# Batched set attention and an MLP on one core: h @ w_in of later batches as one product on four column groups

## The chip, the cores and the metric

The kernel runs on one core of a Trainium2 chip, in one launch. The metric is the device time of an execution in microseconds; for the kernel before it is the median of three runs.

## What is computed

Four batches of 12480 rows go through two attention steps over 32 inducing vectors, and then through an MLP with a gelu in its sigmoid form:

```python
B, N, m, C = (4, 12480, 32, 128)

def mab(q, kv):
    s = scale * (q @ kv.transpose(0, 2, 1))
    s = s - s.max(-1, keepdims=True)
    a = np.exp(s)
    a /= a.sum(-1, keepdims=True) + 1e-09
    return a @ kv
h = mab(I, x)            # (B, 32, 128)
out = mab(x, h)          # (B, 12480, 128)

h1 = out @ w_in          # w_in: 128 x 2048
g = h1 * (1.0 / (1.0 + np.exp(-1.702 * h1)))
result = g @ w_out       # w_out: 2048 x 128
```

## The kernel before

The last product of the second attention and the first of the MLP are joined: the kernel forms `hw = h @ w_in` once a batch (32 x 2048, as four tiles of 512 columns, `hw[b, 0]` to `hw[b, 3]`), and the MLP's first product is then the attention weights times `hw`. To keep float32 precision at the speed of a fast float32 product, weights and `hw` are split into a high and a low part. A tile of `hw` has 128 partitions: the 32 rows of h four times over, the upper two groups the high part, the lower two the low part. A tile of weights, `st`, has the high part in groups 0 and 2 and the low part in 1 and 3, so one product over 128 partitions adds up all four combinations.

**Tiling.** A batch is six super-blocks of 2048 tokens and a remainder of 192 (`sups`, numbers 0 to 6). A block is 512 tokens of one super-block, or the remainders of two batches together (`work`, lines 663 to 683): 98 blocks. Each has eight steps, 784 in all, numbered from 0. A step `first(i)` (684) is two products `ph<-st,hw` on PE, `g` on ACT (gelu), `hi` on ACT or DVE, by which of them has less queued, and `lo` on DVE. `second(i, c)` (711) is three products `pso` with w_out, which follow their step by a lag of up to 12 halves of a step (6 to 12, `LAG`). `ph` has two buffers, so the `ph` products of a step need the gelu of two steps before.

**Order.** Nothing is scheduled by the compiler: each engine runs its instructions in the order in which the program writes them. The main loop (783 to 815) writes one step, then the due `second`s, and then lets two generators run up to their next `yield`: the attention of a later batch (`rest`, line 809), and the laying out of a super-block's weights (`back`). `hop(n)` yields n times, so one yield is one step. `attention(b)` of batch b writes, in this order: the first scores, their maximum and exponentials, the weighted sum, `hT` (the 32 columns of h, four times side by side), the second scores in pairs of super-blocks (`second_products`, 452; `second_out`, 462: a transpose and a reduction on DVE, a subtraction on POOL), first of four super-blocks and then of three, and after each of the two groups their exponentials on ACT. Odd batches begin with their remainder.

Exponentials and gelu need different tables on ACT, so each group of exponentials stands between two table loads. Behind such a group the attention yields LUMP. The main loop then writes `second`s until only 6 halves are left, which gives PE products that need nothing of ACT:

```python
if i < n and next(rest, None) is LUMP:
    while len(under_way) > LAG[0]:
        second(*under_way.pop(0))
    lag, last = LAG[0], i
```

`weights_of(b, s)` (535) normalises the exponentials of a super-block, splits them and copies them to `st` by 32 transfers on SP. Line 772 says from which step on this is due (`begin`): 14 steps before the super-block's first block, earlier where one follows closely. `lay_out` (776) starts it, and where the exponentials are not written by then it runs the attention on:

```python
key = turns.pop(0)
while key not in es:
    next(rest)
return weights_of(*key), key
```

For the first super-block that is laid out in batches 1, 2 and 3 from its own attention's first group, `begin` is 174, 378 and 566.

**Around the change.** `h_w_in(b, c)` (520) is one quarter of `hw`: one product of `hT` (128 columns, h four times) with 512 columns of w_in, a copy to the high part on ACT, a subtraction for the low part on 64 partitions on DVE. For batch 0 the start-up does it; for batches 1 to 3 the list `products` puts the four quarters at single steps shortly before the batch's first block. `phw` is the pool of the tiles of `hw`, `pt` that of the transposed weights. Most instructions carry line 46, that of a helper that records them, so the rows are read by the names of tiles.

Of the kernel before, what the change touches and what calls it, by code (L numbers as in the profile page):

```python
# [8 lines left out]
F32 = mybir.dt.float32  # L9
I32 = mybir.dt.int32  # L10
F32R = mybir.dt.float32r
# [5 lines left out]
P = 128  # L17
# [33 lines left out]
def width(ap):  # L51
    return math.prod(ap.shape[1:])
# [3 lines left out]
def set_attention_then_moe(ctx: ExitStack, tc, xT, x, indT, w_in, w_out, outT):  # L56
    nc = tc.nc
# [11 lines left out]
    dve = Meter(nc.vector, lambda out, *a, **k: 70 + 1.04 * width(out))  # L69
    act = Meter(nc.scalar, scalar_cost)  # L70
    pe_ = Meter(nc.tensor, tensor_cost)
    M = indT.shape[1]
    G = P // M
    DFF = w_in.shape[1]
    NCH = DFF // P
    NG = NCH // 2
    NTOT = xT.shape[1]
    B = 4
# [9 lines left out]
    NS = len(sups)  # L88
# [4 lines left out]
    pe = ctx.enter_context(tc.tile_pool(name="pe", bufs=EB))  # L93
    pt = ctx.enter_context(tc.tile_pool(name="pt", bufs=7))
    pst = ctx.enter_context(tc.tile_pool(name="pst", bufs=G))
    phw = ctx.enter_context(tc.tile_pool(name="phw", bufs=7))
    psm = ctx.enter_context(tc.tile_pool(name="psm", bufs=3))
    ps_h = ctx.enter_context(tc.tile_pool(name="ps_h", bufs=2, space=PSUM))
    ps_o = ctx.enter_context(tc.tile_pool(name="ps_o", bufs=2, space=PSUM))
    ps_a = ctx.enter_context(tc.tile_pool(name="ps_a", bufs=2, space=PSUM))  # L100
# [19 lines left out]
    w_in_sb = const.tile([P, DFF], F32, name="w_in_sb")  # L120
# [4 lines left out]
    hw = {}  # L125
    hTs = {}
    first_h = []
# [21 lines left out]
    def hop(n=4):  # L149

        for _ in range(n):
            yield
# [45 lines left out]
    def attention(b):  # L198

        start = b == 0  # L200
# [44 lines left out]
        def maximum(n):  # L245

            mx1 = psm.tile([P, 1], F32, tag="mx1", name="mx1")
            dve.tensor_reduce(mx1, mx[:, 0:n], axis=AX.X, op=ALU.max)
            yield from wait()
            pa = ps_a.tile([P, 512], F32, tag="pa", name="pa")  # L250
            pe_.matmul(pa[0:1, 0:P], mx1, ident, start=True, stop=True)
            yield
            row = psm.tile([1, G, M], F32, tag="row", name="row")
            dve.tensor_reduce(
                row[:, 0, :], pa[0:1, 0:P].rearrange("p (g m) -> p m g", g=G), axis=AX.X, op=ALU.max
            )
            for j in range(1, G):
                dve.tensor_copy(row[:, j, :], row[:, 0, :])
            yield from wait()
            pa = ps_a.tile([P, 512], F32, tag="pa", name="pa")  # L260
            pe_.matmul(pa[:, 0:1], row.rearrange("p g m -> p (g m)"), one, start=True, stop=True)
            yield
            nmx = psm.tile([P, 1], F32, tag="nmx", name="nmx")
            dve.tensor_scalar(nmx, pa[:, 0:1], -scale, None, op0=ALU.mult)
            yield from wait(2)
            return nmx
# [20 lines left out]
        def weigh(pa, s, xn, i, n):  # L287

            t0, g, w = sups[s]
            q = 32 * g  # L290
            for kk in range(w // 32):
                j = i % G
                pe_.matmul(
                    pa[32 * j:32 * j + 32, 0:P], aTs[s][0:q, kk, :], xn[0:q, kk],
                    start=(i < G), stop=(i >= n - G),
                )
                i += 1
            return i
# [9 lines left out]
        def again(s):  # L308

            if s < NS - 1:  # L310
                load_xT(b, s)

        def blocks(some):
            return sum(sups[s][2] // 32 for s in some)

        if start:
# [36 lines left out]
            def whole():  # L353
                found.append((yield from maximum(NS)))

            whole = whole()
            i = 0
            next(whole)
            spin(SPIN[0])
            for s in range(ES):  # L360
                i = weigh(h1, s, turned[s], i, blocks(range(ES)))
# [17 lines left out]
            i = 0  # L379
            for s in range(ES, NS):  # L380
                if s not in turned:
                    turned[s] = turn_x(b, s)
                i = weigh(h2, s, turned[s], i, blocks(range(ES, NS)))
# [10 lines left out]
        else:  # L394
# [16 lines left out]
            pa = ps_a.tile([P, 512], F32, tag="pa", name="pa")  # L411
# [3 lines left out]
            i = 0  # L415
            for s in range(NS):
# [7 lines left out]
                i = weigh(pa, s, xn, i, blocks(range(NS)))  # L424
# [10 lines left out]
        pa = ps_a.tile([P, 512], F32, tag="pa", name="pa")  # L435
# [16 lines left out]
        def second_products(s):  # L452
            t0, g, w = sups[s]
            pa = ps_a.tile([P, 512], F32, tag="pa", name="pa")
            for j in range(g):
                pe_.matmul(
                    pa[32 * j:32 * j + 32, 0:w], hT[:, 0:M], xts[b, s][:, j * w:(j + 1) * w],
                    start=True, stop=True,
                )
            return pa  # L460

        def second_out(s, pa):

            t0, g, w = sups[s]
            q = 32 * g
            e, slot = take("e", s)
            k = w // 32
            e = e[:, 0:w].rearrange("p (k m) -> p k m", m=M)
            dve.transpose(e[0:q].rearrange("p k m -> p (k m)"), pa[0:q, 0:w])
            m2 = psm.tile([P, BLK], F32, tag="m2", name="m2")  # L470
            dve.tensor_reduce(m2[0:q, 0:k], e[0:q], axis=AX.X, op=ALU.max)
            yield
            eng = dve if start and s == 0 else nc.gpsimd
            eng.tensor_sub(e[0:q], e[0:q], m2[0:q, 0:k].unsqueeze(2).broadcast_to([q, k, M]))  # L474
            yield
            return e, slot
# [8 lines left out]
        if start:  # L485
            for s in range(2):
                pa = second_products(s)
                if s + XB < NS:
                    again(s + XB)
                yield  # L490
                mine[s] = yield from second_out(s, pa)
                exponentials(s, mine[s])
            halves = [h_w_in(b, c) for c in range(DFF // 512)]
            for part in halves:
                next(part)
            spin(SPIN[1])
            yield from weights_of(b, 0)
            for part in halves:
                for _ in part:
                    yield  # L500
            act.activation(warm, one, AF.Gelu_apprx_sigmoid)
            ready.append(True)
        yield
        for some in (turn[2:],) if start else (turn[0:4], turn[4:]):
            yield from hop(20 if start else 8)
# [13 lines left out]

    def h_w_in(b, c):  # L520

        if b == 0:
            if c % 2 == 0:
                first_h.append(ps_h.tile([P, 2, 512], F32, tag="ph", name="ph"))
            pa = first_h[-1][:, c % 2]
        else:
            pa = ps_a.tile([P, 512], F32, tag="pa", name="pa")
        pe_.matmul(pa, hTs[b], w_in_sb[:, c * 512:(c + 1) * 512], start=True, stop=True)
        yield
        t = phw.tile([P, 512], F32R, tag="hw", name="hw")  # L530
        act.copy(t, pa)
        dve.tensor_sub(t[P // 2:P], pa[P // 2:P], t[P // 2:P].bitcast(F32))
        hw[b, c] = t

    def weights_of(b, s):

# [43 lines left out]
    def run(gen):  # L580
        for _ in gen:
            pass
# [78 lines left out]
    first_block = {}  # L661
# [94 lines left out]
            yield from attention(b)  # L756

    n = len(work) * NG

    products = []  # L760
    for b in range(1, B):
        f = first_block[b, NS - 1 if b % 2 else 0] * NG
        products += [(f + at, b, c) for c, at in enumerate((-6, -4, -2, 1) if b % 2 else (-7, -5, -3, -1))]
    rest = attentions()
    act.t = dve.t = pe_.t
    back = part = laid = None
    stores = []
    under_way = []
    turns.pop(0)
# [13 lines left out]
    i, lag, last = 0, LAG[0], 0  # L783
    while i < n or under_way:
        now[0] = i
        if i < n:
            if back is None and turns and i >= begin[turns[0]]:
                back, laid = lay_out()
            while back is not None and first_block[laid] * NG <= i:
                run(back)  # L790
                back = None
                if turns and first_block[turns[0]] * NG <= i:
                    back, laid = lay_out()
            first(i)
            if part is not None:
                run(part)
                part = None
            if products and products[0][0] == i:
                part = h_w_in(*products.pop(0)[1:])
                next(part)  # L800
            under_way += [(i, 0), (i, 1)]
            i += 1
        else:
            lag = 0
        while len(under_way) > lag:
            second(*under_way.pop(0))
        while stores and (stores[0][0] <= i or not under_way):
            nc.sync.dma_start(*stores.pop(0)[1:])
# [4 lines that stand above are left out]
        if lag < LAG[1] and i - last >= EXTRA:  # L813
            lag, last = lag + 1, i
        if back is not None and next(back, 0) == 0:
            back = None
# [33 lines left out]
```

## Time and profile before

| | us |
|---|---|
| median of three runs | 1630.17 (1630.16 to 1631.4) |
| the profiled execution | 1632.7 |
| its span, first to last instruction | 1630.9 |
| PE busy in it | 1591.0 (98%) |
| DVE busy | 1386.9 (85%) |
| ACT busy | 1331.5 (82%) |
| POOL busy | 197.9 (12%) |

The profile's page gives busy times of each engine (PE is the matrix engine, PEld its weight loads, DVE the vector, ACT the scalar, POOL the GpSimd engine, SP the one that issues the transfers), the chain of work that ended last, and groups of instructions. A row of the timeline has the start and the duration in us; instructions of a kind that follow each other are merged in it (x2, x8), and the idle time of the engine just before stands in brackets with what ended it. A product of two plain float32 operands is recorded as two instructions, one of the fast format as one. Times of steps below are program positions; what happens when is read from the timeline.

### The profile page before, as it was taken

To read this page: it belongs to the slowest core of one execution; us is meant where nothing else is said; L and a number is where in the kernel's file an instruction comes from. 1 tells how busy PE (TensorE), PEld (TensorE's weight loads), DVE (VectorE), ACT (ScalarE), POOL (GpSimd) and SP (SyncE) were. 2 spreads that over 40 slices of the span, in tenths; PEclk is the share of its full clock that TensorE was granted. 3 is DMA by queue.
4 is the path that set the end of the run, shared out by engine and by line. 5 is a ranking of instruction groups with operands and counts; after the bars stand their busy time and mean duration, and the time that the engine had idled before them with its cause. 6 is when DMAs were issued, how large, how long until landed. Compare 5 with 4: busy or idle time off the path is not lost.

```text
span 1630.9 us, 21863 instructions
## 1 busy us (share of the span) xinstructions
PE 1591.0 (98%) x7737; PEld 1233.0 (76%) x7737; DVE 1386.9 (85%) x1515; ACT 1331.5 (82%) x1513; POOL 197.9 (12%) x134
## 2 busy tenths in 40 slices
PE   6799999999999999999999999999999999999999
PEld 3477777787777877777766877777777888888887
DVE  7788978988889887888888988878988888889886
ACT  5488888888878878987888878988788888888885
POOL 4311100103101011011120110110121101101100
PEclk9899999999999999999999999999999999999999
DMA  8304219503042112850205101671301011011010
GB/s 338 104 16 175 64 37 203 120 19 97 19 142 76 43 39 56 184 126 20 91 14 202 40 27 39 136 183 40 97 16 42 25 39 46 20 39 46 22 44 20
DMA packets 81947, 126.66 MB, mean 78 GB/s; under 512 B 11632, under 2 KB 50096, under 8 KB 75696
## 3 DMA queue, kind: packets, MB, share of 16 engines
q1 hardware_dynamic: 81840, 125.26, 27.1%
q8 instruction: 63, 1.03, 0.3%
q14 instruction: 44, 0.36, 0.1%
HBM read 74.10 MB, written 25.56 MB: 61 GB/s over the span
## 4 chain that ended last, share of the span: by engine, by line
PE 88%; DVE 4%; ACT 3%; DMA 2%; issue 2%; SPq 1%; POOL 0%; ACTq 0%; DVEq 0%; POOLq 0%
PE pso L46 62%; PE ph L46 22%; PE pa L46 4%; DMA xt<-in_xT 2%; DVE lo L46 2%; ACT g L46 1%; ACT hi L46 1%; SPq L575 1%; DVE sm L46 1%; DVE hi L46 0%; DVE e L46 0%; DVE m L46 0%; DVE hw L46 0%; DVE t L46 0%; ACT s L46 0%
## 5 line engine op out<-in xcount | busy, mean ns | idle before, releaser
L46 DVE TENSOR_TENSOR lo<-g,hi 128x1024 fp32r<-128x1024 f32 (+1 forms) x784 | 983.1, 1268 | 134.4 <-ACT hi L46 122.0
L46 ACT ACTIVATE g<-ph 128x1024 f32<-128x1024 f32 (+1 forms) x784 | 804.3, 1030 | 232.2 <-PE ph L46 119.0
L46 PE MATMUL pso<-hi,wl 128*128 128x512 f32 (+1 forms) x1568 | 623.7, 398 | 0.0
L46 PE MATMUL pso<-hi,wh 128*128 128x512 f32 (+1 forms) x1568 | 617.3, 394 | 0.0
L46 PE MATMUL pso<-lo,wh 128*128 128x512 f32 (+1 forms) x1568 | 616.6, 393 | 0.0
L46 PE MATMUL ph<-st,hw 128*128 128x512 f32 x1536 | 491.2, 401 | 6.8 <-ACT hi L46 2.7
L46 ACT ACTIVATE hi<-ph 128x1024 fp32r<-128x1024 f32 (+1 forms) x464 | 474.1, 1022 | 0.0
L46 PEld LDWEIGHTS ph<-st,hw 128*128 128x128 f32 x1536 | 282.2, 188 | 100.5 <-issue 18.7
L46 PEld LDWEIGHTS pso<-lo,wh 128*128 128x128 f32 x1568 | 294.5, 188 | 73.2 <-issue 2.2
L46 PEld LDWEIGHTS pso<-hi,wl 128*128 128x128 f32 x1568 | 295.3, 188 | 70.4 <-issue 2.9
L46 PEld LDWEIGHTS pso<-hi,wh 128*128 128x128 f32 x1568 | 294.9, 188 | 70.3
L46 DVE CAST hi<-g 128x1024 fp32r<-128x1024 f32 x320 | 239.6, 749 | 77.0 <-ACT g L46 76.7
L547 POOL TENSOR_TENSOR e<-e,sm 128x512 f32<-128x512 f32 (+1 forms) x27 | 44.0, 1631 | 1132.8 <-DVE sm L46 1132.8
L46 ACT COPY ob<-pso 128x512 f32<-128x512 f32 (+1 forms) x98 | 58.0, 591 | 17.5 <-PE pso L46 17.5
L474 POOL TENSOR_TENSOR e<-e,m 128x512 f32<-128x512 f32 (+1 forms) x27 | 42.5, 1574 | 180.4 <-DVE m L46 135.8
L551 POOL TENSOR_TENSOR e<-e,ah 128x512 f32<-128x512 f32 (+1 forms) x27 | 49.5, 1834 | 2.2
L46 PE MATMUL pa<-xt,indT_sb 128*32 128x512 f32 x192 | 27.6, 676 | 17.2 <-DMA xt<-in_xT 17.2
L46 ACT ACT_TABLE_LOAD x28 | 35.9, 1283 | 9.8 <-issue 6.3
L550 POOL CAST ah<-e 128x512 fp32r<-128x512 f32 (+1 forms) x27 | 30.3, 1122 | 1.7
L46 PEld LDWEIGHTS pa<-xt,indT_sb 128*32 128x32 f32 x192 | 4.8, 114 | 28.7 <-issue 15.6
L46 PE MATMUL pa<-xt,hT 128*32 128x512 f32 x192 | 25.5, 637 | 1.0 <-DVE hT L46 1.0
L46 ACT ACTIVATE e<-e 128x512 f32<-128x512 f32 (+1 forms) x28 | 14.2, 572 | 9.5 <-DVE e L46 7.6
(97 smaller groups left out, 452.9 us busy)
## 6 DMA issues: line engine op xcount, KB each, us to landing
xt<-in_xT SPq DMA_DIRECT2D x48, 1024.0 KB, 7.1
out_T<-ob SPq DMA_DIRECT2D x96, 256.0 KB, 2.0
xn<-in_x SPq DMA_DIRECT2D x72, 256.0 KB, 6.8
st<-ahT SPq DMA_DIRECT2D x192, 64.0 KB, 2.0
st<-alT SPq DMA_DIRECT2D x192, 64.0 KB, 2.0
raw<-in_w_in SPq DMA_DIRECT2D x4, 512.0 KB, 8.6
raw<-in_w_out SPq DMA_DIRECT2D x4, 512.0 KB, 7.1
xt_last<-in_xT SPq DMA_DIRECT2D x4, 96.0 KB, 8.2
```

Source lines behind the costliest of these rows:

```text
L46: return f(*a, **k)
L474: eng.tensor_sub(e[0:q], e[0:q], m2[0:q, 0:k].unsqueeze(2).broadcast_to([q, k, M]))
L547: eng.tensor_mul(e[0:q], e[0:q], sm[0:q, 0:nb].unsqueeze(2).broadcast_to([q, nb, M]))
L550: eng.tensor_copy(ah[0:q, 0:w], e2[0:q])
L551: eng.tensor_sub(e2[0:q], e2[0:q], ah[0:q, 0:w].bitcast(F32))
L575: nc.sync.dma_start(st[32 * r:32 * r + 32, at:at + w].bitcast(F32), src[32 * j:32 * j + 32, 0:w])
```

## The change

For batches 1 to 3 the four quarters become one piece of work, right behind `hT`: four products with the 32 columns of h alone, each on another column group of PE and so on another 32 partitions of one PSUM tile; one copy and one subtraction of 128 x 512 for all four; then four transfers for each tile of `hw`, which bring its quarter to the four partition groups, twice from the high part and twice from the low part. The list `products` and what the main loop did with it go. `phw` has 8 buffers instead of 7, `row` one instead of three.

```diff
-    phw = ctx.enter_context(tc.tile_pool(name="phw", bufs=7))
+    phw = ctx.enter_context(tc.tile_pool(name="phw", bufs=8))
...
-            row = psm.tile([1, G, M], F32, tag="row", name="row")
+            row = psm.tile([1, G, M], F32, tag="row", name="row", bufs=1)
...
             act.activation(warm, one, AF.Gelu_apprx_sigmoid)
             ready.append(True)
+        else:
+            yield from hop(4)
+            yield from all_h_w_in(b)
         yield
         for some in (turn[2:],) if start else (turn[0:4], turn[4:]):
...
     def h_w_in(b, c):
 
-        if b == 0:
-            if c % 2 == 0:
-                first_h.append(ps_h.tile([P, 2, 512], F32, tag="ph", name="ph"))
-            pa = first_h[-1][:, c % 2]
-        else:
-            pa = ps_a.tile([P, 512], F32, tag="pa", name="pa")
+        if c % 2 == 0:
+            first_h.append(ps_h.tile([P, 2, 512], F32, tag="ph", name="ph"))
+        pa = first_h[-1][:, c % 2]
...
+    def all_h_w_in(b):
+
+        pa = ps_a.tile([P, 512], F32, tag="pa", name="pa")
+        for c in range(G):
+            pe_.matmul(
+                pa[32 * c:32 * c + 32], hTs[b][:, 0:M], w_in_sb[:, c * 512:(c + 1) * 512],
+                start=True, stop=True,
+            )
+        yield
+        th = pt.tile([P, 512], F32R, tag="t", name="th")
+        act.copy(th, pa)
+        yield
+        tl = pt.tile([P, 512], F32, tag="t", name="tl")
+        dve.tensor_sub(tl, pa, th.bitcast(F32))
+        yield from hop(2)
+        for c in range(G):
+            t = phw.tile([P, 512], F32R, tag="hw", name="hw")
+            for r in range(G):
+                src = th.bitcast(F32) if r < G // 2 else tl
+                nc.sync.dma_start(
+                    t[32 * r:32 * r + 32].bitcast(F32), src[32 * c:32 * c + 32]
+                )
+            hw[b, c] = t
+            yield from hop(2)
...
-    products = []
-    for b in range(1, B):
-        f = first_block[b, NS - 1 if b % 2 else 0] * NG
-        products += [(f + at, b, c) for c, at in enumerate((-6, -4, -2, 1) if b % 2 else (-7, -5, -3, -1))]
...
-            if part is not None:
-                run(part)
-                part = None
-            if products and products[0][0] == i:
-                part = h_w_in(*products.pop(0)[1:])
-                next(part)
```

What it does to the order is seen best at the exponentials of batch 1's first group. On ACT, before, they stand at step 165; `e_3673` and `e_3713` are the scores of its last two super-blocks, `ph` and `g` those of the steps:

```order
L46 ACTIVATE g_3776<-ph_3771 128x1024
L46 ACT_TABLE_LOAD
L46 ACTIVATE e_3524<-e_3524 64x96
L46 ACTIVATE e_3562<-e_3562 128x512
L46 ACTIVATE e_3673<-e_3673 128x512
L46 ACTIVATE e_3713<-e_3713 128x512
L46 COPY ob_3796<-pso_3664 128x512
L46 ACT_TABLE_LOAD
L46 ACTIVATE g_3816<-ph_3811 128x1024
```

All of them stand behind the gelu of step 164, `g_3776`. On DVE, before, the last transpose and reduction that they need are written ahead of the `lo` of three earlier steps, those of `g_3722`, `g_3738` and `g_3757`:

```order
L46 STREAM_TRANSPOSE e_3713<-pa_3650 128x512
L46 TENSOR_REDUCE m2_3715<-e_3713 128x16
L46 TENSOR_TENSOR lo_3721<-g_3722,hi_3720 128x1024
L46 CAST hi_3736<-g_3738 128x1024
L46 TENSOR_TENSOR lo_3737<-g_3738,hi_3736 128x1024
L46 TENSOR_REDUCE sm_3748<-e_1308 64x3
L46 TENSOR_SCALAR sm_3748<-sm_3748 64x3
L46 RECIPROCAL sm_3748<-sm_3748 64x3
L46 TENSOR_TENSOR lo_3756<-g_3757,hi_3755 128x1024
```

So the last reduction is several steps old when ACT comes to the exponentials. With the change the same exponentials stand on ACT at step 174, where `lay_out` asks for them; the last two super-blocks are now `e_3960` and `e_3965`:

```order
L46 ACTIVATE g_3935<-ph_3930 128x1024
L46 ACTIVATE hi_3933<-ph_3930 128x1024
L46 COPY ob_3945<-pso_3800 128x512
L46 ACT_TABLE_LOAD
L46 ACTIVATE e_3833<-e_3833 64x96
L46 ACTIVATE e_3871<-e_3871 128x512
L46 ACTIVATE e_3960<-e_3960 128x512
L46 ACTIVATE e_3965<-e_3965 128x512
L46 ACT_TABLE_LOAD
L46 ACTIVATE g_3979<-ph_3974 128x1024
```

So the group has moved from the gelu of step 164 to that of step 173. On DVE, with the change, the transposes and reductions stand between `lo` of that same step before and `hi` of the step behind:

```order
L46 TENSOR_TENSOR lo_3934<-g_3935,hi_3933 128x1024
L46 STREAM_TRANSPOSE e_3960<-pa_3948 128x512
L46 TENSOR_REDUCE m2_3962<-e_3960 128x16
L46 STREAM_TRANSPOSE e_3965<-pa_3953 128x512
L46 TENSOR_REDUCE m2_3967<-e_3965 128x16
L46 CAST hi_3977<-g_3979 128x1024
L46 TENSOR_TENSOR lo_3978<-g_3979,hi_3977 128x1024
```

No step's `hi` or `lo` is left between the last reduction and the exponentials that need it. And on PE the pair of second products (`pa_3948`, `pa_3953`) stands just ahead; the `ph` behind the ten rows here is `ph_4013`, which takes the buffer of `ph_3974`:

```order
L46 MATMUL pa_3948<-xt_2539,hT_3285 32x512 x4
L46 MATMUL pa_3953<-xt_2688,hT_3285 32x512 x4
L46 MATMUL ph_3974<-st_3611,hw_728 128x512 x2
L46 MATMUL pso_3983<-hi_3841,wl_108 128x512
L46 MATMUL pso_3983<-lo_3842,wh_107 128x512
L46 MATMUL pso_3983<-hi_3841,wh_107 128x512
L46 MATMUL pso_3983<-hi_3841,wl_108 128x512
L46 MATMUL pso_3983<-lo_3842,wh_107 128x512
L46 MATMUL pso_3983<-hi_3841,wh_107 128x512
L46 MATMUL ph_3994<-st_3611,hw_728 128x512 x2
```

Before, PE has 24 `pso` products between two `ph` pairs at each of the 13 LUMPs behind the start-up; with the change at ten of them, and 6 at steps 174, 378 and 566. At step 566 the order is that of step 174; at step 378 three of the four super-blocks have had their turn on DVE and POOL by then, and the fourth has its subtraction next to the exponentials.

## Rows read from the trace of the kernel before

**Rows 1.** The page, parts 1 and 4: busy time, and the chain by engine.
```profile
PE 1591.0 (98%) x7737; PEld 1233.0 (76%) x7737; DVE 1386.9 (85%) x1515; ACT 1331.5 (82%) x1513; POOL 197.9 (12%) x134
PE 88%; DVE 4%; ACT 3%; DMA 2%; issue 2%; SPq 1%; POOL 0%; ACTq 0%; DVEq 0%; POOLq 0%
```

**Rows 2.** Waits of PE: us in total, times, longest us.
```profile
PE pa L46 <- DMA xt<-in_xT: 17.2, 7, 8.2
...
PE ph L46 <- ACT hi L46: 2.7, 6, 1.1
...
PE ph L46 <- ACT g L46: 2.3, 2, 1.3
```

**Rows 3.** Timeline of PE around two quarters of h @ w_in.
```profile
445.81 0.63 PE L46 MATMUL ph<-st,hw 128*128 128x512 f32 x2
446.28 1.02 PE L46 MATMUL pa<-w_in_sb,hT 128*128 128x512 f32 x2
...
447.36 0.39 PE L46 MATMUL pso<-lo,wh 128*128 128x512 f32 x1
...
454.25 0.63 PE L46 MATMUL ph<-st,hw 128*128 128x512 f32 x2
...
456.42 0.39 PE L46 MATMUL pso<-lo,wh 128*128 128x512 f32 x1
```

**Rows 4.** Timeline of PE around second products, two sets and one.
```profile
383.70 1.92 PE L46 MATMUL pa<-xt,hT 128*32 128x512 f32 x16
385.56 0.73 PE L46 MATMUL ph<-st,hw 128*128 128x512 f32 x2
...
431.24 1.07 PE L46 MATMUL pa<-xt,hT 128*32 128x512 f32 x8
432.24 0.73 PE L46 MATMUL ph<-st,hw 128*128 128x512 f32 x2
432.80 0.39 PE L46 MATMUL pso<-hi,wl 128*128 128x512 f32 x1
```

**Rows 5.** SP: timeline of its issues, its longest wait, the page's part 6.
```profile
377.23 0.58 SPq L575 DMA_DIRECT2D st<-ahT  x1
377.87 0.59 SPq L575 DMA_DIRECT2D st<-alT  x1
...
SPq L808 <- ACT ob L46: 963.3, 93, 19.0
...
st<-ahT SPq DMA_DIRECT2D x192, 64.0 KB, 2.0
```

**Rows 6.** Timeline of ACT over the exponentials at step 165.
```profile
398.49 1.28 ACT L46 ACT_TABLE_LOAD   x1
399.79 1.85 ACT L46 ACTIVATE e<-e 64x96 f32<-64x96 f32 x4
401.54 0.56 ACT L46 COPY ob<-pso 128x512 f32<-128x512 f32 x1
403.55 1.28 ACT L46 ACT_TABLE_LOAD   x1 [1.44 <-issue]
404.84 1.94 ACT L46 ACTIVATE g<-ph 128x1024 f32<-128x1024 f32 x2
```

**Rows 7.** Timeline of DVE and POOL over second scores; POOL's group on the page.
```profile
833.04 0.70 DVE L46 STREAM_TRANSPOSE e<-pa 128x512 f32<-128x512 f32 x1
833.85 0.69 DVE L46 TENSOR_REDUCE m<-e 128x16 f32<-128x512 f32 x1
834.46 1.22 DVE L46 TENSOR_TENSOR lo<-g,hi 128x1024 fp32r<-128x1024 f32 x1
...
834.68 1.89 POOL L474 TENSOR_TENSOR e<-e,m 128x512 f32<-128x512 f32 x1 [2.64 <-DVE m L46]
...
L474 POOL TENSOR_TENSOR e<-e,m 128x512 f32<-128x512 f32 (+1 forms) x27 | 42.5, 1574 | 180.4 <-DVE m L46 135.8
```

**Rows 8.** PE's timeline; stretches with length, busy us of PE and others, clock, DMA.
```profile
483.24 1.94 PE L46 MATMUL pa<-xt,indT_sb 128*32 128x512 f32 x8 [2.77 <-DMA xt<-in_xT]
...
482.40:489.25 6.85, 6.01 (x19) 3.95 (x20) 0.91 (x1) 2.51 (x4) 0.00 (x0) 0.50 0.54 228
840.70:844.20 3.50, 2.19 (x10) 1.46 (x9) 3.50 (x3) 2.30 (x3) 3.21 (x2) 1.00 0.20 75
```

More of the change, by code (lines that the diff above doesn't have):

```diff
@@ L758, in set_attention_then_moe @@
     n = len(work) * NG
-    products = []
-    for b in range(1, B):
-        f = first_block[b, NS - 1 if b % 2 else 0] * NG
-        products += [(f + at, b, c) for c, at in enumerate((-6, -4, -2, 1) if b % 2 else (-7, -5, -3, -1))]
     rest = attentions()
     act.t = dve.t = pe_.t
-    back = part = laid = None
+    back = laid = None
     stores = []
```

## The prediction

> **What bounds the kernel now.** I read the page first: PE is busy 98% of the span and carries 88% of the chain that ended last [rows 1]. The reader is to see there that ACT (82%) and DVE (85%) have room, so that whatever shortens PE's queue of work shortens the time, and whatever makes PE stand still lengthens it. The waits of PE say how well it is fed: after the start-up only one wait is large, 17.2 us for loads of `xt`, and waits of `ph` for ACT come to 5.0 us in the whole run [rows 2]. Then I read single stretches: the product that the change replaces, the work that resembles its replacement, and one "lump", where ACT leaves its gelu for exponentials.
>
> **What the change removes and adds on PE.** A full product of 512 columns takes a slot of 0.234 us on PE (445.81 to 446.28 holds two). From the start of a product `pa<-w_in_sb,hT` to the start of the second `pso` behind it 1.08 us pass, where 0.23 would without it: 0.85 us each [rows 3]. Two of the twelve also wait for their buffer: 454.25 to 456.42 is 2.17 us where 0.70 would do, 1.47 each. Ten at 0.85 and two at 1.47 are 11.4 us. The four parts on the four column groups are, for PE, what `second_products` does for one super-block: the same 32 columns of `hT`, four groups, 512 columns. Two such sets take 1.85 us up to the next `ph`, one takes 1.00 [rows 4], and the `ph` pair behind it 0.56 instead of 0.47. So 1.1 us a batch, 3.3 in all, and PE is relieved of 8.1 us. Were the four parts to run one behind the other, they would cost 3.4 a batch, and that bounds the gain below at about 1 us.
>
> ACT makes 3 copies instead of 12 and DVE 3 subtractions instead of 12. Neither bounds, so I count nothing; the cover is PE's own work, and if it were gone 5 us on each engine would count in favour of the change. The larger pool and the single buffer of `row` cost nothing: `row` is next written a batch later, and a slot of `hw` is written again only when its batch's blocks are over.
>
> The SP queue gets 16 transfers of 64 KB a batch. An issue takes 0.63 us there (377.23 to 377.87), so 10 us; one lands after 2.0. SP waits 963 us in all for outputs alone [rows 5], so the queue has room, and `hw` itself is not read for some 30 steps. The `st` copies of the next super-block stand behind the first 12 (7.6 us). I price that at nothing, since their tiles are read by PE only some steps later; what it costs if that cover is gone is a rival below.
>
> **What the change moves.** This is the part that decides. `all_h_w_in` puts 16 yields between `h` and the second scores: 4, 1, 1, 2 and four times 2. One yield is one step, so all that follows in that batch's attention comes 16 steps later. Before, the first four super-blocks got their exponentials at steps 165, 365 and 557. Their weights fall due (`begin`) at 174, 378 and 566. 16 steps later is 181, 381 and 573: too late in each of three batches. Then `lay_out` drives the attention on by itself, without the hops, until the exponentials are issued. Two things follow, and the order shows both. The exponentials stand right behind the transposes and subtractions that they need; and the LUMP that the attention yields is taken by `lay_out`'s own loop, so the main loop does not run PE's 18 products ahead. The other lumps keep theirs.
>
> What a lump costs ACT is in the rows: from the first table load at 398.49 to the gelu at 404.84 are 6.3 us [rows 6]. PE does not stand still there: 18 extra products, 4.2 us, and two ordinary steps of 1.87 are in front of the `ph` that needs ACT again. Without the 18, PE has the two steps alone.
>
> At 174 and 566, counted from T, the start of the pair of sets on PE:
> - PE: pair to 1.85, two steps of 1.87 to 5.6. The next `ph` needs the gelu of step 174.
> - ACT: `g` of the step before starts when its `ph` pair ends, T - 1.87 + 0.63; `g` and `hi` at 0.97 each end at T + 0.7, the copy of `ob` (0.56) at 1.3, the table load (1.28) at 2.6, the two exponentials that are ready at 3.4.
> - DVE: `lo` (1.22) waits for that `hi` and ends at 2.0; transpose, reduction (0.81 from start to start, 0.69) [rows 7] end at 3.5, those of the second super-block at 4.9.
> - POOL subtracts at 1.57 us in the mean and 1.89 beside a busy DVE: from 3.6 the two end at 6.8 or 7.4.
> - ACT again: last exponential 0.6, table load 1.28, `g` 1.0, and 0.1 on the way: 9.8 or 10.4.
>
> PE stands 4.2 to 4.8 us; I take 4.5, as DVE has a pause in that stretch. At 378 only the last of the four super-blocks is late. From U, the start of that step's `ph`: `g` and `hi` of the step before end at 0.7, table load at 2.0, three exponentials at 3.6; the fourth's reduction ends near 1.6 and its subtraction at 3.5, so ACT is hardly held up: 4.2, table load 5.5, `g` 6.5. PE arrives after two steps, 3.7: 2.8 us (2.2 if `hi` of that step is off ACT's path). Together 11.8 us.
>
> **The clock.** The only fall of PE's clock after start-up stands behind the wait of 2.77 us (with 0.56 just before) at 483: from 482.40 to 489.25 the granted clock is 0.50, that is 1.2 instead of 2.4 GHz, with PE busy 6.01 us of it [rows 8]. Half of that, 3.0 us, is what it cost. In the other direction, from 840.70 to 844.20 PE is idle 1.31 us of 3.50 and the clock stays at 1.00. The two long stalls lie beyond the first of these: 3.0 each. The short one is as long as the 2.77 but has no second wait at its side; between nothing and 3.0 I take 1.5, as it may go either way. That makes 7.5 (0 to 9).
> The Trainium skill has a rule that speaks against this change: "TensorE: Matmul & The Clock Gate", section "HAM oscillation", has it that a PE which waits between bursts falls back to the slow clock and begins its next burst there. By that rule all three stalls pay, and the sum would be 1.5 us higher; the row at 482.40 agrees with it, and the stretch at 840.70 shows a wait that did not.
>
> **Sum.** -8.1 + 11.8 + 7.5 = +11.2 us. The waits for the first `xt` of batches 2 and 3 also shift, by the new order of SP's queue and of the lump before them: from 1.1 less to 3 more, taken as nothing. Against the profiled execution's own 1632.7 us that is 1643.9; the median of the runs is 2.5 us lower, so 1641.4.
>
> **The rivals.**
> - A, the forecast: three uncovered lumps with falls of the clock, 1641.4. Chance 0.64.
> - B, the same stalls while the clock stays: -8.1 + 11.8, 1633.9. For it speaks the stretch at 840.70, against it that the waits here are two to three times as long. 0.18.
> - C, on the other side: the late lump stays covered, because ACT gets back to its gelu before PE has used up its two steps. The place is the `ph` two steps behind the forced one, and it decides at 5.6 us behind T (3.7 behind U): if ACT's chain is shorter, nothing is lost and PE's relief alone counts, 1622.1. For it: ACT and DVE have 15 to 18% of room. Against it: ACT alone, with nothing late, took 6.3 us over a lump that began when its own step was done. 0.12.
> - D: SP's queue becomes the bound. If the `st` copies behind the transfers come after the product that reads them, PE waits up to 10 us at three places, up to 1672. It decides when the copies of a super-block's first tile land later than its first step begins. SP's 963 us of waiting speak against it. 0.04. The Trainium skill ("DMA: Bandwidth & Descriptors", "Rules for kernel authors") advises to coalesce many small transfers, which this change does not; nothing here is worked out from it.
> - E: the change does not do on PE what it says, and the four parts run one behind the other: 6.9 us more, 1648.3. The sets of rows 4 overlap, so 0.02.
>
> **How the numbers follow.** About 0.2%, 3.3 us, is what a measurement of this kernel can tell from no change: 1626.9 to 1633.4. Slower are A (0.64), half of B (0.09), D and E (0.06): 0.79. The other half of B and a little of C are the same: 0.10. The rest of C is faster: 0.11. The range, 1628 to 1648, takes in A with its bounds (-1.1, +3 and the clock's 0 to 9), B, and leaves out most of C and D. Slower cases alone hold 1633.5 to 1648.
>
> **What would show it.** In the changed profile: products of `w_in` on PE as 32 columns, some 1 us a batch. PE waits for ACT's `g` of 4 us and more near steps 174 and 566, and of 2 to 3 near 378; behind them stretches of a granted clock of 0.50. ACT's `e` waiting for POOL at the two long places. `pso` products 6, not 24, between the `ph` pairs there. I am wrong if PE runs through these places without a wait over 1.5 us, or if the waits are there but the time is still below that of before, which would mean that the removed work was worth more than 11.4 us.

## The result, and the profile after

| us | before | with the change |
|---|---|---|
| median of 20 runs each | 1629.82 | 1632.79 |
| ratio, with its 95% interval | | 1.0017 (1.0011 to 1.0024) |
| the profiled execution | 1632.7 | 1634.04 |
| its span | 1630.9 | 1632.2 |

The change makes the kernel slower by about 3 us, some 0.2%. That is the forecast direction and lies in the forecast range, but it is a quarter of the +11.2 us that the sum gave, and slightly less than the bound of 0.2% that the forecast itself set for "no change".

The page of the changed kernel, part 1 and one group of part 5, beside [rows 1] and the last of [rows 7]:

```profile
PE 1590.0 (97%) x7737; PEld 1236.2 (76%) x7737; DVE 1374.5 (84%) x1512; ACT 1323.2 (81%) x1498; POOL 195.6 (12%) x134
...
L474 POOL TENSOR_TENSOR e<-e,m 128x512 f32<-128x512 f32 (+1 forms) x27 | 39.9, 1477 | 180.6 <-DVE m L46 176.0
```

PE is busy 1 us less in a span 1.3 us longer. Busy time alone can't tell why, as instructions at the lower clock count as longer ones. The waits of PE (total, times, longest) are clearer, beside [rows 2]:

```profile
PE pa L46 <- DMA xt<-in_xT: 14.9, 4, 8.0
PE ph L46 <- ACT g L46: 10.7, 4, 3.4
...
PE ph L46 <- ACT hi L46: 1.4, 3, 0.9
```

Waits for ACT's `g` went from 2.3 to 10.7 us: these are the three stalls that the forecast is about. Two other rows fell: `xt` from 17.2 to 14.9, and waits for `hi` from 2.7 to 1.4. Most of the time for `xt` stands in the start-up, before 31 us: 13.0 before and 12.5 after. Behind it are 4.2 and 2.5, so the forecast's reading that the 17.2 us come after the start-up was wrong.

PE's timeline around the new product, at batch 1 (it looks the same at 764.15 and 1151.91):

```profile
360.87 0.39 PE L46 MATMUL pso<-hi,wh 128*128 128x512 f32 x1
361.19 1.06 PE L46 MATMUL pa<-w_in_sb,hT 128*32 128x512 f32 x8
362.18 0.73 PE L46 MATMUL ph<-st,hw 128*128 128x512 f32 x2
362.75 0.40 PE L46 MATMUL pso<-hi,wl 128*128 128x512 f32 x1
```

From `pso` to `pso` are 1.88 us, where an ordinary `ph` pair has 0.70 (a slot of 0.23 and 0.47): 1.18 us a batch. The four parts do run side by side.

PE's timeline at the three places, steps 174, 378 and 566 (in brackets: idle before, and what ended it):

```profile
421.16 0.39 PE L46 MATMUL pso<-hi,wh 128*128 128x512 f32 x1
424.77 0.73 PE L46 MATMUL ph<-st,hw 128*128 128x512 f32 x2 [3.22 <-ACT g L46]
...
832.25 0.39 PE L46 MATMUL pso<-hi,wh 128*128 128x512 f32 x1
836.05 1.22 PE L46 MATMUL ph<-st,hw 128*128 128x512 f32 x2 [3.42 <-ACT g L46]
...
1211.88 0.39 PE L46 MATMUL pso<-hi,wh 128*128 128x512 f32 x1
1215.34 1.22 PE L46 MATMUL ph<-st,hw 128*128 128x512 f32 x2 [3.07 <-ACT g L46]
```

The idle times in the brackets come to 9.7 us. From the start of the last `pso` to the start of the `ph` behind it, 0.23 us pass where nothing waits, so the first stall costs 424.77 - 421.16 - 0.23 = 3.38; the others, likewise, 3.57 and 3.23: 10.2 us in all. The forecast had 4.5, 2.8 and 4.5. All three are of one size, and the "short" one is the longest.

ACT, POOL and DVE at step 174. The pair of second products starts on PE at 415.72, the forecast's T:

```profile
416.86 1.28 ACT L46 ACT_TABLE_LOAD   x1
418.15 0.81 ACT L46 ACTIVATE e<-e 64x96 f32<-64x96 f32 x2
420.28 0.63 ACT L46 ACTIVATE e<-e 128x512 f32<-128x512 f32 x1 [1.32 <-POOL e L474]
421.76 0.63 ACT L46 ACTIVATE e<-e 128x512 f32<-128x512 f32 x1 [0.85 <-POOL e L474]
422.40 1.28 ACT L46 ACT_TABLE_LOAD   x1
423.70 1.94 ACT L46 ACTIVATE g<-ph 128x1024 f32<-128x1024 f32 x2
...
419.19 1.05 POOL L474 TENSOR_TENSOR e<-e,m 128x512 f32<-128x512 f32 x1 [5.51 <-DVE m L46]
420.67 1.05 POOL L474 TENSOR_TENSOR e<-e,m 128x512 f32<-128x512 f32 x1 [0.43 <-DVE m L46]
...
419.84 0.69 DVE L46 TENSOR_REDUCE m<-e 128x16 f32<-128x512 f32 x1
```

The chain is the forecast one: the last reduction is done by 420.53, POOL subtracts, ACT waits for it twice, then the last exponential, the table load and `g`. But POOL takes 1.05 us for a subtraction, not 1.57 to 1.89, as DVE rests beside the second one and has only a transpose and a reduction beside the first. So `g` ends 9.0 us behind T and not at 9.8 to 10.4.

The same at step 378, where U, the start of the step's `ph`, is 828.77:

```profile
829.59 1.28 ACT L46 ACT_TABLE_LOAD   x1
830.88 1.68 ACT L46 ACTIVATE e<-e 128x512 f32<-128x512 f32 x3
833.03 0.63 ACT L46 ACTIVATE e<-e 128x512 f32<-128x512 f32 x1 [0.48 <-POOL e L474]
833.68 1.28 ACT L46 ACT_TABLE_LOAD   x1
834.98 1.94 ACT L46 ACTIVATE g<-ph 128x1024 f32<-128x1024 f32 x2
...
826.57 1.90 POOL L474 TENSOR_TENSOR e<-e,m 128x512 f32<-128x512 f32 x1 [8.80 <-DVE m L46]
831.10 1.90 POOL L474 TENSOR_TENSOR e<-e,m 128x512 f32<-128x512 f32 x1 [2.64 <-DVE m L46]
...
827.75 1.80 DVE L46 TENSOR_TENSOR lo<-g,hi 128x1024 fp32r<-128x1024 f32 x1 [0.20 <-ACT hi L46]
...
830.27 0.69 DVE L46 TENSOR_REDUCE m<-e 128x16 f32<-128x512 f32 x1
```

Here POOL's last subtraction does take 1.90 us, as priced, and ACT waits for it 0.48 us. The forecast had ACT "hardly held up" and took the exponentials to end at U + 4.2; they end at 833.66, U + 4.9. What came late is the reduction: it ends at U + 2.2 and not near 1.6. The `lo` ahead of it on DVE started while POOL was still at the subtraction for the third super-block, and took 1.80 us where 1.22 is usual.

The clock, in stretches of PE's timeline (length, busy us of PE and the others, granted clock, DMA):

```profile
426.10:429.50 3.40, 3.40 (x10) 2.62 (x9) 3.30 (x7) 1.65 (x3) 1.96 (x3) 0.50 0.00 0
835.70:839.10 3.40, 3.05 (x7) 2.47 (x8) 2.96 (x6) 2.24 (x3) 0.00 (x0) 0.50 0.02 5
1214.60:1221.40 6.80, 6.06 (x14) 4.84 (x15) 5.91 (x9) 3.97 (x5) 2.49 (x3) 0.50 0.00 0
...
487.60:491.00 3.40, 3.40 (x14) 2.07 (x7) 0.00 (x0) 1.27 (x2) 0.00 (x0) 0.51 1.06 406
```

Behind each of the three stalls the granted clock is 0.50, that is 1.2 GHz, as forecast; but for 3.4, 3.4 and 6.8 us. Half of PE's busy time there is taken as lost, as in the forecast: 1.7, 1.5 and 3.0, together an estimate of 6.2 us where the forecast had 7.5. Behind the `xt` wait of batch 2 the low clock lasts 3.4 us now (1.7 lost); before it was 6.85 with PE busy 6.01, 3.0 lost [rows 8].

Between the same two program points, steps 100 and 750, the two profiled executions differ by only +0.5 us (of the rest, +1.2 stand ahead of it and -0.4 behind). Counted from the brackets of PE's timeline and from half the busy time in stretches at 0.50: idle time of PE +5.1 (the three stalls +9.7, all other waits -4.6), low clock +4.9 (6.2 at the stalls, -1.3 at the `xt` wait), so that -9.5 is left for PE's work. Of that, 2.0 belong to the one execution of before: its 150 steps from 600 to 750, which hold no wait and run at a granted clock of 1.00, take 280.0 us, and the same steps of the kernel before with six more yields (the last experiment) take 278.0. So about -7.5 is left. The forecast had -7.4 for that work (-8.1 with 0.7 of waits for `hw`), 11.8 and 7.5. Single profiles are a weak scale: that of before lies 2.9 us above its median, that of the change 1.25 above. The experiments therefore go by medians.

### The profile page after: what moved, and what is told of

It is laid out like the page before. It is cut to its first block, busy times and chain, and to the rows that moved or that the text cites. A ratio compares the mean times of both kernels' runs of the same rounds, so it can differ in the third digit from the quotient of the medians.

```text
span 1632.2 us, 21897 instructions
## 1 busy us (share of the span) xinstructions
PE 1590.0 (97%) x7737; PEld 1236.2 (76%) x7737; DVE 1374.5 (84%) x1512; ACT 1323.2 (81%) x1498; POOL 195.6 (12%) x134
## 4 chain that ended last, share of the span: by engine, by line
PE 89%; DVE 5%; ACT 2%; DMA 2%; issue 1%; POOL 1%; SPq 0%; ACTq 0%; DVEq 0%; POOLq 0%
PE pso L46 63%; PE ph L46 22%; PE pa L46 4%; DVE lo L46 2%; DMA xt<-in_xT 2%; ACT g L46 1%; ACT hi L46 1%; DVE e L46 0%; DVE hi L46 0%; DVE m L46 0%; DVE sm L46 0%; ACT L46 0%; DVE t L46 0%; ACT s L46 0%; POOL e L474 0%
## 5 line engine op out<-in xcount | busy, mean ns | idle before, releaser
L46 PE MATMUL ph<-st,hw 128*128 128x512 f32 x1536 | 492.9, 402 | 13.3 <-ACT g L46 10.7
L46 ACT ACTIVATE hi<-ph 128x1024 fp32r<-128x1024 f32 (+1 forms) x458 | 467.5, 1021 | 0.0
L46 DVE CAST hi<-g 128x1024 fp32r<-128x1024 f32 (+1 forms) x326 | 237.9, 730 | 83.9 <-ACT g L46 83.7
L46 PE MATMUL pa<-xt,indT_sb 128*32 128x512 f32 x192 | 26.1, 647 | 15.0 <-DMA xt<-in_xT 14.9
L575 POOL CAST ah<-e 128x512 fp32r<-128x512 f32 (+1 forms) x27 | 34.2, 1266 | 1.7
```

Of the source, the lines that this page charges most:

```text
L46: return f(*a, **k)
L575: eng.tensor_copy(ah[0:q, 0:w], e2[0:q])
```

## Experiments

The theory was: the late exponentials, which `lay_out` forces at steps 174, 378 and 566 and which swallow the LUMP, cost stalls and clock; the new form of the product is a gain. The rivals: the late place costs by itself, through the chain over DVE and POOL; or the gain is small, and the form is worth nothing. Differences are of medians in us, and ratios are against runs of the kernel before beside them, whose medians were 1631.16 for the first four, 1629.54 for the next three and 1629.34 for the last two.

### Seven yields in place of sixteen

```diff
-            yield from hop(4)
             yield from all_h_w_in(b)
...
-        yield from hop(2)
+        yield
         for c in range(G):
...
-            yield from hop(2)
+            yield
```

> The change with 7 yields between h and the second scores instead of 16 (no hop(4) in front, one yield instead of hop(2) in four places and in the middle). Nothing else differs; the exponentials of batches 1 to 3 come at steps 172, 372 and 564, before they fall due, and keep their LUMP. Theory 'late' (the change's loss is the three groups of exponentials that lay_out forces): PE's waits of 3.2 to 3.6 us for ACT's g and the clock's falls behind them go, so about 10 + 5 us less than the change: 1617 to 1622 us, 8 to 13 us below before. Rival 'small relief' (the new product saves little, since its transfers and the moved scores cost what it frees, and the stalls are mostly made up for later): within 2 us of the change, 1630 to 1635.

Measured: 1621.35, ratio 0.994 (0.9925 to 0.9954). The exponentials now stand at steps 172, 372 and 564, ahead of the deadline, and the LUMPs are kept. That is within what the lateness theory expected. In the waits of PE nothing of the stalls is left:

```profile
PE pa L46 <- DMA xt<-in_xT: 17.6, 7, 8.0
...
PE ph L46 <- ACT g L46: 1.5, 2, 1.0
```

What is left stands at the first `xt` of batch 2, in PE's timeline:

```profile
481.72 1.93 PE L46 MATMUL pa<-xt,indT_sb 128*32 128x512 f32 x8 [3.75 <-DMA xt<-in_xT]
```

and in the stretch around it:

```profile
480.20:490.40 10.20, 8.15 (x26) 3.88 (x27) 1.88 (x4) 2.90 (x4) 0.00 (x0) 0.50 1.02 423
```

Everything else of the change is still there, and the kernel beats both others. So nine steps of lateness, and nothing of the new product, make the change slow: 11.4 us lie between this kernel and the change. The wait for `xt` in batch 2 is worse here, 3.75 us in one piece, and the low clock around it lasts 10.2 us.

### The late place, with the LUMP kept

```diff
         while key not in es:
-            next(rest)
+            if next(rest) is LUMP:
+                lumps.append(key)
...
+            if lumps:
+                lumps.clear()
+                while len(under_way) > LAG[0]:
+                    second(*under_way.pop(0))
+                lag, last = LAG[0], i
             first(i)
```

> The change with one difference: where lay_out drives the attention on and meets LUMP, the main loop writes PE's 18 extra products there too, ahead of the step. The exponentials stay as late as in the change. Theory 'late', with the missing 4.2 us of products as the cause: the waits of 3.2 to 3.6 us shrink to under 0.5 and the clock stays, 1617 to 1623. Rival (the chain through DVE and POOL is the cause, not the missing products; PE then reaches ACT as late as before): half of the stall stays, 1626 to 1631. 'Small relief': 1630 to 1635.

Measured: 1624.74, ratio 0.9958 (0.9943 to 0.9974). The same 16 yields leave the exponentials to `lay_out` as in the change, but PE has its 18 products. The stalls of 3.1 to 3.4 us are gone. In the waits of PE, and in its timeline of batches 1 and 3, smaller ones stand in front of the `left` blocks:

```profile
PE ph L46 <- ACT g L46: 4.2, 3, 1.6
...
456.59 0.69 PE L46 MATMUL ph<-left,hw 128*128 128x192 f32 x4 [0.92 <-ACT hi L46]
...
469.38 0.69 PE L46 MATMUL ph<-left,hw 128*128 128x192 f32 x4 [1.64 <-ACT g L46]
...
1253.68 0.88 PE L46 MATMUL ph<-left,hw 128*128 128x192 f32 x4 [1.64 <-ACT g L46]
```

Some eight of the 11.4 us come back by the cover alone. That is between the two ranges, 1617 to 1623 and 1626 to 1631, and nearer to the first. PE is idle 10.0 us here between steps 100 and 750, and 6.5 with seven yields, so the new waits go with what is missing. The missing cover is the cause of the stalls; the chain over DVE and POOL sets how long a stall lasts once the cover is gone. The same is seen inside the change: at step 378, where three of four super-blocks were in time and ACT waits for POOL only 0.48 us, the stall is as long as at the others.

The expectation that the clock stays was wrong at one place:

```profile
1254.00:1257.40 3.40, 3.40 (x15) 3.40 (x14) 3.33 (x5) 1.84 (x3) 0.00 (x0) 0.50 0.42 100
```

The wait of 1.64 us at 1253.68 is followed by 3.4 us of the low clock, and the same wait at 469.38 is not.

### The late place, with the old quarters

```diff
-        pa = ps_a.tile([P, 512], F32, tag="pa", name="pa")
-        for c in range(G):
-            pe_.matmul(
...
         for c in range(G):
+            pa = ps_a.tile([P, 512], F32, tag="pa", name="pa")
+            pe_.matmul(pa, hTs[b], w_in_sb[:, c * 512:(c + 1) * 512], start=True, stop=True)
+            yield
...
-                nc.sync.dma_start(
...
+            act.copy(t, pa)
+            dve.tensor_sub(t[P // 2:P], pa[P // 2:P], t[P // 2:P].bitcast(F32))
```

> The change with the old four quarters (128 columns, four products one behind the other, low part written on 64 partitions, no transfers) at the new place, with the same 16 yields. Only the form of the product differs from the change. If the new form relieves PE by 8 to 10 us, this is 8 to 10 us above the change: 1640 to 1643. 'Small relief' (transfers and drains take back what the column groups give): 1632 to 1636.

Measured: 1637.9, ratio 1.0041 (1.0027 to 1.0056): 5.1 us above the change by medians, 3.8 by the differences to before. That is below what was expected (8 to 10) and above the rival's range. The form is a gain, but this run gives it with an uncertainty of some 2 us.

### Idle yields in the kernel before

```diff
             ready.append(True)
+        else:
+            yield from hop(16)
```

> The kernel before, with 16 idle yields between h and the second scores and nothing else: the quarters of h @ w_in stay where they were. The exponentials are forced at 174, 378 and 566 as in the change. Theory 'late': the three stalls and the clock's falls without the relief, 10 to 15 us above before: 1640 to 1645. Rival 'small relief': the delay costs about as much as the whole change, 1631 to 1635.

Measured: 1660.16, ratio 1.0177 (1.0161 to 1.0192), a miss of 15 us. The stalls for `g` are there (11.8 us), and others that nobody had expected, for the buffers of `pa`: 10.8 us for `hw` and 3.8 for `e`. So the delay was tried again with 8 yields, at which nothing is forced:

> The kernel before with 8 idle yields between h and the second scores; the quarters stay where they were. The exponentials come at 173, 373 and 565, one step before they fall due, and keep their LUMP. Theory: what costs in the run with 16 yields is the forcing (PE's waits for ACT's g) and the quarters meeting the second scores in the two buffers of pa, not the delay itself; with 8 yields PE has no wait for g over 1.5 us there and the time is within 4 us of before (1627 to 1634). Rival: a delay of the second scores costs by itself, in proportion to its steps, so half of what 16 cost: some 14 us, 1643 to 1647.

Measured: 1650.44, ratio 1.0133 (1.0115 to 1.0152), again a miss, above the rival's 1643 to 1647 too. Its waits of PE show no stall for `g`, but six for `pa` until DVE has subtracted:

```profile
PE pa L46 <- DVE hw L46: 12.8, 6, 4.2
...
PE ph L46 <- ACT g L46: 1.0, 1, 1.0
```

PE's timeline at the first of the two longest:

```profile
447.05 0.40 PE L46 MATMUL pso<-hi,wh 128*128 128x512 f32 x1
451.68 1.94 PE L46 MATMUL pa<-xt,hT 128*32 128x512 f32 x8 [4.24 <-DVE hw L46]
```

and the stretch behind it, with the granted clock at 0.50:

```profile
450.70:457.50 6.80, 5.82 (x17) 3.34 (x18) 4.65 (x5) 1.99 (x3) 1.94 (x2) 0.50 0.00 0
```

The quarters at their old place use the two `pa` buffers, one each, and free them only when DVE has subtracted. Second scores that come later meet them there and wait up to 4.24 us for a buffer. So this pair does not measure "lateness alone": delay and the old place of the quarters collide. The change avoids that by moving the quarters away as well, which the forecast didn't see.

### Seven yields, with the old quarters

The edit is that of the old quarters above, made to the kernel with seven yields.

> The kernel with 7 yields, with the old four quarters (128 columns, no transfers) in place of the new product, at the new place and with 7 yields: nothing is forced. Against the kernel with 7 yields only the form of the product differs: 4 x 0.85 - 1.1 = 2.3 us a batch, 7 in all, so 1627 to 1630 us. Against before only the place differs: the waits around the old place (for ACT, for hw's buffer, for xt) go, 1 to 4 us. Rival (the gain of the 7 yields' kernel is the place, not the column groups): within 2 us of that kernel, 1620 to 1624.

Measured: 1628.06, ratio 0.9993 (0.9984 to 1.0002), as expected. Against the kernel with seven yields and the new form the form is worth 6.7 us by medians, 8.3 by the differences to before. The profiles of both pairs agree with the slots' 6.7: PE's own work between steps 100 and 750, with idle time and half of the low clock taken off, is 7.0 us longer with the old quarters at sixteen yields and 6.9 at seven. The new place by itself brings 1 to 2 us at most.

### Time for the xt loads

The wait for the first `xt` of batches 2 and 3, which the forecast took "as nothing", was then taken out of the way: six yields between the first loads and their use, in the kernel with seven yields, in the change and in the kernel before.

```diff
             for s in range(XB):
                 load_xT(b, s)
                 yield
+            yield from hop(6 if b > 1 else 0)
```

> The kernel with 7 yields, with 6 more yields between the first loads of xt of batches 2 and 3 and the first scores; its later steps stay where they are. PE's wait for xt at batch 2 (3.7 us in one piece) and batch 3 goes. If the clock's fall behind it (10.2 us at half in that kernel's profile) comes from PE standing still there, it goes too: 4.3 us of idle time and 3 to 4 us of slow clock, 1613 to 1616 us. Rival (the clock falls there for another reason, or the wait moves elsewhere): 1617 to 1621, with a stretch of 0.50 still near 480 to 490 us.

Measured: 1612.72, ratio 0.99 (0.9883 to 0.9918), 0.3 us under the expected range. The two halves of its span behind the start-up:

```profile
80.00:840.00 760.00, 759.67 (x3740) 586.56 (x3740) 656.15 (x708) 643.76 (x724) 95.30 (x60) 1.00 0.32 86
840.00:1609.00 769.00, 765.98 (x3539) 606.96 (x3539) 658.33 (x686) 641.59 (x713) 75.02 (x48) 1.00 0.22 61
```

The clock is 1.00 throughout, and PE is idle 3.4 us of 1529. This version beats the kernel before by 1.0% and the change by 1.2%.

> The change with 6 more yields between the first loads of xt of batches 2 and 3 and the first scores, all else as in the change: the exponentials are still forced at 174, 378 and 566. The wait for xt at batch 2 and the clock's fall behind it go (2.5 and 1.7 us in the change's profile): 1628 to 1629 us. Against the kernel with 7 yields and the same 6 (1612.7) nothing differs but the forcing, so the gap is the whole price of the three stalls and of the clock behind them: 16 us (10 of waits and 6 of clock). Rival: the stalls are mostly made up for later by PE's backlog, and the gap stays the 11 us that the two kernels without the 6 yields show: 1624.

Measured: 1627.3, ratio 0.9991 (0.9982 to 1.0), 0.7 us under what was expected; the gap of 14.6 to the kernel with seven yields lies between the 16 and the rival's 11. Its three stalls are those of the change, 3.22, 3.42 and 3.07 us. Stretches behind the three (length, busy us, clock, DMA):

```profile
423.60:427.00 3.40, 3.40 (x10) 2.66 (x9) 3.26 (x7) 1.50 (x2) 1.09 (x2) 0.50 0.00 0
829.80:836.60 6.80, 5.67 (x13) 4.47 (x14) 5.55 (x8) 3.96 (x5) 2.43 (x2) 0.50 0.01 2
...
1210.30:1220.00 9.70, 9.70 (x42) 7.82 (x43) 9.49 (x14) 8.13 (x9) 2.50 (x3) 1.00 0.01 3
```

PE's timeline at the third:

```profile
1210.29 0.74 PE L46 MATMUL ph<-st,hw 128*128 128x512 f32 x2 [3.07 <-ACT g L46]
```

A stall of 3.07 us was followed by the low clock in the change and was not in this kernel.

> The kernel before with the same 6 yields ahead of the first scores of batches 2 and 3. The waits for xt there (3.3 and 0.9 us) and the clock's fall (3.0) go: 1622 to 1624 us. If so, the change made on this kernel (the run above against this one) costs 5 to 7 us instead of 3: the rest was given back by shorter waits for xt. Rival: the waits for xt have no part in it, and the change costs 3 us here too.

Measured: 1623.26, ratio 0.9965 (0.9952 to 0.9979). The change is 4.0 us slower than before when neither waits for `xt`, and 3.0 when both do. Between "5 to 7" and the rival's 3 this doesn't decide, as each interval is some 2 us wide to either side.

The three runs with `xt` out of the way split the change:

- product and place, nothing forced (before to seven yields): 1612.72 - 1623.26 = -10.5, with an uncertainty of some 3.5 us by the two intervals;
- nine more steps of lateness (seven yields to the change): 1627.3 - 1612.72 = +14.6, with some 3 us;
- sum +4.0; with the `xt` waits back it is +3.0, so about 1 us is given back there, which is inside the uncertainty.

The profiles of the first pair say what its gain is made of. Steps 100 to 750, in the kernel before and then with seven yields, both with six more yields (length, busy us, clock, DMA):

```profile
267.87:1545.08 1277.21, 1273.26 (x6067) 997.37 (x6066) 1105.57 (x1170) 1075.45 (x1206) 141.86 (x93) 1.00 0.26 71
268.57:1535.91 1267.34, 1265.64 (x6068) 993.21 (x6066) 1096.62 (x1163) 1070.74 (x1196) 147.58 (x93) 1.00 0.28 74
```

With the clock at 1.00 in both, 9.9 us are saved: 7.6 of PE's own work, and 2.25 of idle time, which falls from 3.95 to 1.70.

## Why the prediction was right and wrong

**Right.** What bounds the kernel, the mechanism and its three places. The exponentials became late, `lay_out` forced them, the LUMP was swallowed, PE stood still in front of the `ph` two steps behind, the clock fell, and the kernel got slower. That the lateness is the cause is shown (seven yields), and that it acts through the lost cover is shown too (the LUMP kept). Of the signs named, the sizes missed: 3.22 and 3.07 us where 4 and more were to be seen, and 3.42 where 2 to 3 were. Rival C (the lump stays covered), D (SP's queue) and E (parts one behind the other) are excluded by rows of the change: three waits, none of PE for `st`, 1.18 us a product. No wait of PE shows a cost of SP's 16 transfers. That the saved work on DVE and ACT counts for nothing was not tested by itself; it fits that PE's slots alone give the form's 6.7.

**Wrong.** The size: +3.0 and not +11.2. The step that failed is the price of the late lumps, the stalls and the clock behind them: 19.3 us in the sum, 14.6 measured, more than the uncertainty. Two smaller terms were off in the same direction, each within the uncertainty, and the result is a small difference of two larger numbers:

- *The stalls, 11.8; measured 10.2.* The POOL term was mis-sized. It was priced by the mean of all subtractions (1.57, a group of two shapes; 128x512 alone has 1.71) and by a row beside a busy DVE (1.89), while in a forced lump DVE is through with its own work: 1.05 us. That makes the long stalls 3.4 and 3.2 and not 4.5. Against it the short one was 3.6 and not 2.8: the `lo` lengthened by POOL, 1.80 for 1.22, made the reduction late, and ACT waited for it.
- *The clock, 7.5; measured 6.2 in the change's profile, and some 4.5 in the one with `xt` out of the way* (half of 3.40 and 5.67). The price of 3.0 a fall came from the single row that there was. A fall after such a stall lasts 3.4 or 6.8 us, and of the six in these two kernels one had none. Where rival B had the clock stay, it gave 1633.9; that the time came out near it is luck, since the clock did fall.
- *The relief, -8.1; measured -10.5 by medians and -9.9 by the profiles.* The step that removes 12 slots of 0.85 us and adds 3 products of 1.1 was right: 12 x 0.85 - 3 x 1.18 = 6.7, and the old quarters with seven yields gave 6.7 to 8.3. PE's work fell by 7.6, of which some 0.7 is not the form's. The idle time fell by 2.25: 0.7 for the two waits for a buffer, which the forecast had at 1.2, and the rest mostly short waits for `hi`, which it didn't count. The row with 1.31 us of idle in front of a `ph` [rows 8] is gone in the change, but with seven yields 0.27, 0.52 and 0.40 us stand some steps behind that place instead.
- *The `xt` waits, "from 1.1 less to 3 more, taken as nothing"; measured about 1 less by medians.* In the two profiles it is more: 1.7 us of waits and 1.3 of the low clock. By these the bound below was too narrow, as it had no term for the clock at that place.

In sum, by medians: 4.7 less for stalls and clock, 2.4 more relief, 1.1 given back: 8.2 us, from +11.2 to +3.0.

The Trainium skill states a rule that bears on the POOL term ("Trainium Architecture — The Big Picture", "What this means for kernel authors"): DVE and GpSimd contend for one shared pair of ports, which one of them holds at a time. The rows agree: a subtraction takes 1.05 us alone and 1.90 when a `lo` is already under way, and a `lo` that starts while POOL is at it takes 1.80. For the clock, the Trainium skill's rule weighed ahead of the result ("TensorE: Matmul & The Clock Gate", "HAM oscillation"), that a PE which waits between bursts begins its next one on the slow clock, fits all three stalls of the change, and not the one at 1210.29 in the change with six more yields. The Trainium skill ties this to waits that are long enough, a condition that the forecast left out when it had all three stalls pay.

Still open: why a stall of the same length is followed by 3.4 us of the low clock, by 6.8, or by none; no run here varied that alone. Over the 20 runs of the change the time and the mean granted clock (0.987 to 0.993) go together with a correlation of -0.81, so the falls go with much of the scatter. Also open is the exact share of the `xt` waits, which lies inside the intervals.

## What to carry to other kernels

A change that adds yields to a cooperative schedule has two prices: its work, and what comes later because of it. Look up each deadline and what cover is lost when it is missed, and try the same change with fewer yields, which here turned +0.2% into -0.6%, and into -1% with the loads moved too. When a forecast is the difference of two larger terms, size both from stretches that look like the future ones (here a POOL row beside an idle DVE), and read every wait that stands around the place that is vacated.

## What was not expected of the hardware

- A POOL subtraction of 128x512 takes 1.05 us while DVE rests or does reductions, and 1.90 beside a `lo`. The one that starts second is the longer: at 831.10 in the change POOL starts inside a `lo`, which still takes 1.22 us, and at 827.75 a `lo` starts inside POOL's subtraction and takes 1.80.
- The low clock comes in stretches of 3.4, 6.8 and 10.2 us, and their length doesn't follow from that of the wait: 3.07 us of idle gave 6.8 in one kernel and none in another, 3.42 gave 3.4 and 6.8, and 1.64 gave 3.4 and none within one execution.
- With two buffers for `pa`, eight idle yields ahead of the second scores cost 21 us without any forced lump: 13.9 us of waits for those buffers in its profile, where other users hold them, and three stretches of 6.8 us of the low clock behind.
